# One fixed list of steps for all four batches of an attention and Fourier-mixing kernel

## Chip, core and metric

The kernel runs on one core of one Trainium2 chip. The metric is the device time of one execution in microseconds. Before the change the median of three runs is 622.02 us (621.33 to 622.77). The profiled execution took 623.03 us; its span, from the first to the last instruction, is 621.2 us.

## What is computed

Gated linear attention over 4 batches of 8 heads (768 tokens, 48 channels each), then a Fourier mixing block on the heads laid side by side (384 channels), a normalisation and two projections (384 to 1536 to 384).

```python
f = 1.0 / (1.0 + np.exp(-f_logit))
for t in range(S):
    state = f[:, :, t, :, None] * state + np.einsum('bhd,bhe->bhde', k[:, :, t], v[:, :, t])
    y[:, :, t] = np.einsum('bhd,bhde->bhe', q[:, :, t], state)
...
X = np.fft.fft(np.fft.fft(x, axis=1), axis=2)
u = x + np.real(X).astype(np.float32)
un = (u - mu) / np.sqrt(var + 1e-06)
ch = np.maximum(un @ w_ch1, 0.0) @ w_ch2
return (u + ch).astype(np.float32)
```

The weights arrive as 64-bit numbers and are turned into 32-bit ones on the chip.

## The kernel before

**Attention** works on 16 units of two heads each, four to a batch: `u = 4 b + hp`. A unit is a Python generator (`attention`, then `outputs`, then `fold`) of 13 steps, and each call of `next` records one of them:

1. `expln`: two ACT functions on the gate g;
2. DVE's scan of the gates over the tokens (L277) and the small `deep`;
3. three ACT exponentials;
4. the products of q and of k with them on DVE (L289, L290);
5. the scores `sc` on PE (L303);
6. their masking on DVE (L310, `at`);
7. `st`: k turned by PE (L448) and copied out by ACT;
8. `ds`: the states' increments on PE (L459);
9. DVE's scan of the states (`stt`, L467);
10. and 11. the outputs `y` on PE (L479, L486), copied out by ACT;
12. `yt`: turned by PE (L505) and copied by ACT into the batch's x;
13. `fold`: sums and differences of x on DVE and POOL, the input of the Fourier step. For a batch's last unit (hp = 3) all of it is on DVE.

**fnet** takes one batch: four products `z` with the table of cosines (L587), `mid` and three `mix` products (L618, L603) with their additions into x, and for each of 6 tiles of 128 tokens the moments, the normalised tile `un` (L636) and its turning `pt` on PE (L639), copied into `unT`. z, mid, mix and the first three pt are called the front of a batch here. Then the projections follow in two halves of 3 tiles: 12 groups `up` (L671, each with a Relu on ACT into h) and 3 tiles `po` (L681, 12 matmuls of 128x384 each, which read all 12 h), an addition into x (L685) and the store.

**Stores.** Tiles 0 and 4 of a batch go to the output by SP's DMA queue (L563); tile 4 in two pieces, of 1 row and of 127 rows. Tiles 1, 2, 3 and 5 go by an indirect DMA of POOL (L557), whose target rows are not known to the recording layer, so each store waits for the one before it.

**Weights.** 24 blocks of 384 KB of words (`raw`, three buffers) are loaded by SP (L235) and converted by two DVE steps (L198, L199), two ACT steps (L208, L209) and an addition of POOL (L211). `size_of` (L259) loads each block a second time and takes the smallest magnitude in it; the 24 minima, with two figures of the attention, decide a flag. If the flag is set, all is computed again by slower steps in a branch at the program's end.

**What sets the order.** Each engine runs its instructions in one order. Up to the middle of batch 0's projections that order is the list ORDER: a digit is one step of that unit, C converts a block, F is one step of fnet, L a load, T the loads of the cosine tables, S their sorting. After it a loop over PATTERN steps three units at a time and puts between them whole pieces of fnet: four up groups at a time, a whole po tile. fnet of a batch can only be called when the one before has ended. The flag is computed at the end (L760 to L770), behind the last po.

PE has two PSUM buffers for z, mix, pt, up and po together, two for sc, st, ds and yt, and one for y.

Of the kernel before, what the change touches and what calls it, by code (L numbers as in the profile page):

```python
# [19 lines left out]

PATTERN = ((2, 0), (1, 0), (1, 1), (1, 0), (2, 1), (2, 0), (1, 0), (1, 1), (1, 0),
           (0, 1), (0, 0), (0, 0), (-1, 1))
# [5 lines left out]

ORDER = (
# [8 lines left out]
def kernel(  # L38
# [105 lines left out]
    def tables():  # L144


        nc.sync.dma_start(out=tab[:, 0], in_=seq_tab[:, 0])
# [8 lines left out]
        nc.sync.dma_start(out=tab[0:1, 0, 1], in_=seq_tab[64:65, 1, 1])  # L156
# [73 lines left out]
    raws, done = [], [0]  # L230
# [24 lines left out]
    def size_of(i):  # L255


        if wide:
            nc.vector.tensor_reduce(small[:, i:i + 1], words(i)[:, :, 1].bitcast(F32), mybir.AxisListType.X,  # L259
                                    ALU.min, apply_absolute_value=True)  # L260

    def attention(u, x_all):
# [28 lines left out]
        if u:  # L291
            load(u + 3, "f", "k")
# [145 lines left out]
    def outputs(u, x_all, AT, Q, K, te, T=None):  # L438
# [61 lines left out]
        load(u + 4, "q", "v")  # L500
# [3 lines left out]
        for c, i in enumerate((0, 1, 4, 2, 3, 5)):  # L504
            nc.tensor.transpose(ps[:, c * 128:c * 128 + R], to[:, i], ident[:R, :R])  # L505
        nc.scalar.copy(
            x_all[:, :, hp * 2 * D:(hp + 1) * 2 * D].rearrange("t c (r e) -> t c r e", r=2),
            ps[:, :NCH * 128].rearrange("t (c r k) -> t c r k", r=2, k=64)[:, :, :, :D])
        yield
        fold(u, x_all)  # L510
# [53 lines left out]

    def fnet(b, x, again=False):
# [13 lines left out]
        for T in (1, 3, 0, 2):  # L579
# [11 lines left out]
            yield True  # L591
# [40 lines left out]
        unT = p2.tile([128, 3, 3 * 128], F32, tag="unT", name=f"unT{b}_0")  # L632

        def turn(c):
            un = p2.tile([128, DM], F32, tag="un", name=f"un{b}_{c}")
# [4 lines left out]
            nc.scalar.copy(unT[:, :, c % 3 * 128:(c % 3 + 1) * 128],  # L640
                           pt[:, :DM].rearrange("p (k t) -> p k t", k=3))

        for c in range(3):
# [5 lines left out]
            if c == 0:  # L649
                nc.vector.tensor_copy(x[0:1, 3], row[0:1])  # L650
            else:
                turn(c - 1)
            yield True
        turn(2)
        yield True

        for half in range(2):
            if half:
                for c in range(3, NCH):
                    moments(c)  # L660
                deviation(slice(3, NCH))
                unT = p2.tile([128, 3, 3 * 128], F32, tag="unT", name=f"unT{b}_1")
                for c in range(3, NCH):
                    turn(c)
            h1 = []
            for m in range(NF):
                if b == 1 and not again:
                    size_of(half * NF + m)
# [7 lines left out]
                yield m % 4 == 3  # L676
            for i in range(3):
                c = 3 * half + i
                po = ps_f.tile([128, 512], F32, tag="f", name=f"po{b}_{c}")
                for m in range(NF):  # L680
                    nc.tensor.matmul(po[:, :DM], lhsT=h1[m][:, i * 128:(i + 1) * 128], rhs=w2[:, m],  # L681
                                     start=(m == 0), stop=(m == NF - 1))
                    if c == 0 and m in (3, 7):
                        yield False
                nc.vector.tensor_tensor(x[:, c], po[:, :DM], x[:, c], ALU.add)  # L685
                store(b, c, x[:, c])
                yield True

    x_of, units, behind = {}, {}, []
    steps = [0] * (B * HP)

    def step(u):
        if not 0 <= u < B * HP:
            return
        b, hp = divmod(u, HP)
        if u not in units:
            if b not in x_of:  # L700
                x_of[b] = p2.tile([128, NCH, DM], F32, tag="x", name=f"x{b}")
            units[u] = attention(u, x_of[b])
        steps[u] += 1
        if units[u] and next(units[u], units) is units:
            units[u] = None
            if hp == HP - 1:
                behind.append(fnet(b, x_of.pop(b)))

    def fill(n=1, small_steps=False):

        while n and behind:
            ended = next(behind[0], None)
            if ended is None:
                behind.pop(0)
            elif ended or small_steps:
                n -= 1

    tile_of = {"g": g_t, "k": k_t, "q": q_t}
    with tc.manual_schedule():
        for word in ORDER.split():  # L720
            kind = word[0]
            if kind.isdigit():
                step(int(word))
            elif kind == "F":
                fill(1, small_steps=True)
            elif kind == "C":
                weights()
            elif kind == "R":
                fetch(int(word[1:]))
            elif kind == "L":  # L730
                load(int(word[1]), *word[2:])
            elif kind == "G":
                gap(*(tile_of[name[0]][int(name[1])] for name in word[1:].split(",")))
# [14 lines left out]
    for u, n in ((k - 2, 10), (k - 1, 4), (k, 1)):  # L748
        while steps[u] < n:
            step(u)  # L750
# [104 lines left out]
```

## Time and profile before

| what | us | share of the span |
|---|---|---|
| profiled execution, its own time | 623.03 | |
| its span | 621.2 | 100% |
| PE busy (3450 matmul records) | 554.5 | 89% |
| PE's weight loads, beside the matmuls | 361.4 | 58% |
| DVE busy | 239.4 | 39% |
| ACT busy | 195.2 | 31% |
| POOL busy | 100.7 | 16% |
| bytes moved by DMA | 44.27 MB | |

A product of 32-bit numbers shows as two matmul records, a turning as one. Matmul ends are modelled, so records overlap a little; lengths are therefore taken from pieces in which the same kind of matmul runs without a break. PE and PEld name the matmuls and the weight loads of the same engine. "Granted clock" is the share of TensorE's full clock that was granted.

### The profile page before, as it was taken

Reading aid. Unit: us, or ns where it says so; the run is one execution under the profiler, and the core shown is the slowest. Engines: PE = TensorE matmul, PEld = TensorE weight load, DVE = VectorE, ACT = ScalarE, POOL = GpSimd, SP = SyncE. Lnnn points to the kernel's source line nnn. Section 1 sums busy time; section 2 is a strip of 40 time slices with the busy share of each in tenths; the row PEclk is TensorE's granted clock in tenths of the full one; section 3 lists DMA queues with packets and bytes.
Section 4 is the critical chain, followed back from the end, with each engine's and each line's share of the span. In section 5 each row is a group of like instructions: output and inputs, shape, how many; then the busy total and the mean of one; then the engine's idle time right before and its main releaser. Section 6 shows DMA issues by size and latency. Waiting matters only on the chain.

```text
span 621.2 us, 8567 instructions
## 1 busy us (share of the span) xinstructions
PE 554.5 (89%) x3450; PEld 361.4 (58%) x3450; DVE 239.4 (39%) x431; ACT 195.2 (31%) x441; POOL 100.7 (16%) x147
## 2 busy tenths in 40 slices
PE   2865769997999979999999998999999969999993
PEld 1655546654556767655655677656655645555551
DVE  7869896209234587700420359201200350000000
ACT  5766556533311446420321224310221022102200
POOL 5445232225000113300210101100100000000000
PEclk9997788999899979999999999999999988999998
DMA  8959373323880343101100100000000000000000
GB/s 234 254 163 237 100 199 114 112 89 104 274 256 18 109 126 89 46 0 33 45 0 20 35 24 1 1 0 26 15 1 14 13 14 0 1 25 13 1 13 31
DMA packets 18113, 44.27 MB, mean 71 GB/s; under 512 B 2958, under 2 KB 4304, under 8 KB 18064
## 3 DMA queue, kind: packets, MB, share of 16 engines
q1 hardware_dynamic: 16960, 40.09, 22.8%
q0 software_dynamic: 1104, 3.54, 1.5%
q8 instruction: 29, 0.48, 0.3%
q14 instruction: 20, 0.16, 0.1%
HBM read 38.90 MB, written 4.72 MB: 70 GB/s over the span
## 4 chain that ended last, share of the span: by engine, by line
PE 73%; DVE 11%; DMA 9%; issue 3%; ACT 1%; POOL 1%; SPq 1%; POOLq 0%; DVEq 0%; ACTq 0%
PE up L671 31%; PE po L681 26%; PE z L587 3%; DMA raw<-in_w_ch_dram 3%; PE mix L603 2%; PE y L479 2%; DVE W L277 2%; DMA g<-in_qkf_dram 2%; PE sc L303 2%; PE y L486 2%; DMA out_dram<-x 2%; PE pt L639 2%; DMA tab<-in_seq_tab_dram 1%; DVE at L310 1%; PE yt L505 1%
## 5 line engine op out<-in xcount | busy, mean ns | idle before, releaser
L671 PE MATMUL up<-unT,w 128*128 128x384 f32 x576 | 195.5, 499 | 1.1 <-ACT unT L640 1.1
L681 PE MATMUL po<-w,h 128*128 128x384 f32 x576 | 189.2, 488 | 0.0
L671 PEld LDWEIGHTS up<-unT,w 128*128 128x128 f32 x576 | 110.8, 195 | 78.2 <-issue 5.7
L681 PEld LDWEIGHTS po<-w,h 128*128 128x128 f32 x576 | 108.7, 190 | 74.8 <-issue 1.1
L685 DVE TENSOR_TENSOR x<-po,x 128x384 f32<-128x384 f32 x24 | 13.4, 557 | 252.2 <-PE po L681 252.2
L674 ACT ACTIVATE h<-up 128x384 f32<-128x384 f32 x96 | 47.0, 490 | 133.7 <-PE up L671 133.7
L557 POOL DMA_INDIRECT out_dram<-x,place x16 | 17.0, 1060 | 354.5 <-DVE x L685 301.2
L303 PE MATMUL sc<-q,W 48*64 48x128 f32 x768 | 32.4, 296 | 22.6 <-DVE W L290 17.1
L303 PEld LDWEIGHTS sc<-q,W 48*64 48x64 f32 x768 | 26.3, 145 | 25.5 <-DVE W L290 13.9
L211 POOL TENSOR_TENSOR w<-w,raw 128x384 uint32<-128x384 uint32 x24 | 28.9, 1204 | 53.9 <-ACT raw L209 34.4
L310 DVE COPY_PREDICATED at<-causal,sc 128x768 f32<-128x768 uint32 x32 | 31.6, 1026 | 14.3 <-PE sc L303 14.0
L479 PE MATMUL y<-at,v 128*64 128x128 f32 (+1 forms) x384 | 31.3, 300 | 1.1 <-ACT yT L499 0.7
L479 PEld LDWEIGHTS y<-at,v 128*64 128x64 f32 (+1 forms) x384 | 25.7, 145 | 6.3 <-issue 4.5
L277 DVE TENSOR_TENSOR_SCAN W<-g,bound 112x768 f32<-112x768 f32 x16 | 27.9, 1747 | 1.9 <-issue 1.0
L450 ACT COPY kT<-st 128x560 f32<-128x560 f32 x16 | 10.0, 627 | 51.0 <-PE st L448 50.8
L639 PE MATMUL pt<-ident,un 128*128 128x128 f32 x72 | 13.8, 319 | 12.1 <-DVE un L636 8.9
L495 ACT COPY yT<-y 112x254 f32<-112x254 f32 x16 | 5.8, 364 | 57.3 <-PE y L486 57.3
L467 DVE TENSOR_TENSOR_SCAN stt<-ds,te 112x288 f32<-112x288 f32 x16 | 12.0, 751 | 27.7 <-PE ds L459 27.7
L640 ACT COPY unT<-pt 128x384 f32<-128x384 f32 x24 | 11.2, 478 | 35.1 <-PE pt L639 35.0
L486 PE MATMUL y<-q,stt 48*48 48x128 f32 x320 | 21.4, 276 | 0.8 <-DVE stt L467 0.8
L259 DVE TENSOR_REDUCE small<-raw 128x1 f32<-128x384 f32 x24 | 13.1, 551 | 21.5 <-DMA raw<-in_w_ch_dram 21.5
L486 PEld LDWEIGHTS y<-q,stt 48*48 48x48 f32 x320 | 18.1, 159 | 5.3 <-issue 3.0
(116 smaller groups left out, 525.2 us busy)
## 6 DMA issues: line engine op xcount, KB each, us to landing
raw<-in_w_ch_dram SPq DMA_DIRECT2D x48, 384.0 KB
v<-in_v_dram SPq DMA_DIRECT2D x16, 288.0 KB
g<-in_qkf_dram SPq DMA_DIRECT2D x32, 144.0 KB
k<-in_qkf_dram SPq DMA_DIRECT2D x32, 144.0 KB
q<-in_qkf_dram SPq DMA_DIRECT2D x32, 144.0 KB
out_dram<-x SPq DMA_DIRECT2D x4, 192.0 KB
out_dram<-x SPq DMA_DIRECT2D x4, 190.5 KB
tab<-in_seq_tab_dram SPq DMA_DIRECT2D x1, 386.0 KB
```

The source lines that it names most:

```text
L211: nc.gpsimd.tensor_tensor(bits, bits, lo, ALU.add)
L277: nc.vector.tensor_tensor_scan(W, g, bound[:R], 0.0, ALU.add, ALU.min)
L303: nc.tensor.matmul(ps[64 * s:64 * s + 64, r, i * C:(i + 1) * C], lhsT=W[ROWS[r], o + 64 * s:o + 64 * s + 64], rhs=Q[ROWS[r], o:o + C], sta ...
L310: nc.vector.copy_predicated(AT[:, :, half], causal.bitcast(U32).unsqueeze(1).unsqueeze(1).to_broadcast([128, 2, NCH // 2, C]), ps[:, :, :N ...
L479: nc.tensor.matmul(y[FILL[r], c * C:(c + 1) * C], lhsT=vt[:, c, r * D:r * D + (64 if r == 0 else D)], rhs=AT[:, r, c], start=(c % 4 == 0), ...
L486: nc.tensor.matmul(y[ROWS[r], c * C:(c + 1) * C], lhsT=st[ROWS[r], :, c - 1], rhs=Q[ROWS[r], c * C:(c + 1) * C], start=False, stop=True, s ...
L557: nc.gpsimd.indirect_dma_start(out=out.rearrange("b s d -> (b s) d"), out_offset=bass.IndirectOffsetOnAxis(ap=place[:, b, i:i + 1], axis=0 ...
L587: nc.tensor.matmul(z[:, cols], lhsT=src[:, j, lo:hi], rhs=tab[:, t, T % 2, cols], start=(i == 0), stop=(i == len(parts) - 1), skip_group_c ...
L639: nc.tensor.transpose(pt[:, kt * 128:(kt + 1) * 128], un[:, kt * 128:(kt + 1) * 128], ident)
L671: nc.tensor.matmul(pp[:, :3 * 128], lhsT=w1[:, kt, m * 128:(m + 1) * 128], rhs=unT[:, kt], start=(kt == 0), stop=(kt == 2))
L674: nc.scalar.activation(h, pp[:, :3 * 128], AF.Relu)
L681: nc.tensor.matmul(po[:, :DM], lhsT=h1[m][:, i * 128:(i + 1) * 128], rhs=w2[:, m], start=(m == 0), stop=(m == NF - 1))
```

## The change

ORDER now holds the whole program, 533 words, and PATTERN with its loop is gone. Its words name the batch (F0 to F3), and fnet is cut finer: every up group is a step, and every po tile three. The turnings are a generator of their own (H), the minima a word (c) that reads the block already loaded for the conversion and then issues the next block's load, and every load is a word (L). The flag is a word (M).

```diff
+    "Gq0 L0v Gq2 Gk2 Gq3 I L0f 0 Gk1 Gk0 L1f L0q Gq1 0 L1k i 1 L0k R Z 0 L1q 1 0 1 C C L3fk c 0 0 0 L2f "
...
@@ tables
-        nc.sync.dma_start(out=tab[:, 0], in_=seq_tab[:, 0])
+        nc.sync.dma_start(out=tab[:, 0, 0], in_=seq_tab[:, 0, 0])
+        nc.sync.dma_start(out=tab[1:128, 0, 1], in_=seq_tab[1:128, 0, 1])
+        nc.sync.dma_start(out=tab[0:1, 0, 1], in_=seq_tab[64:65, 1, 1])
...
@@ weights, sizes
             single(dst, raws[i])
-            fetch()
...
+    def sizes():
+        i = looked[0]
         if wide:
-            nc.vector.tensor_reduce(small[:, i:i + 1], words(i)[:, :, 1].bitcast(F32), mybir.AxisListType.X,
+            nc.vector.tensor_reduce(small[:, i:i + 1], raws[i][:, :, 1].bitcast(F32), mybir.AxisListType.X,
                                     ALU.min, apply_absolute_value=True)
+            fetch()
+        looked[0] += 1
...
@@ attention, outputs
-        if u:
-            load(u + 3, "f", "k")
...
-        load(u + 4, "q", "v")
+        if te is None:
+            load(u + 4, "q", "v")
...
@@ fnet
+        def turns():
+            for c in range(NCH):
+                if c == 3:
+                    for i in range(3, NCH):
+                        moments(i)
+                    deviation(slice(3, NCH))
+                    yield
+                turn(c)
+                yield
+
+        behind[b] = turns()
...
-                if b == 1 and not again:
-                    size_of(half * NF + m)
...
-                yield m % 4 == 3
-            for i in range(3):
+                yield
+            for i in ((0, 1, 2), (0, 2, 1))[half]:
...
-                    if c == 0 and m in (3, 7):
-                        yield False
+                    if m in (3, 7):
+                        yield
...
@@ the end
+            elif kind == "M":
+                flag = judge()
     tc.no_sync_barrier()
-    k = 6
-    while steps[k - 2] >= 13 and steps[k - 1] >= 10 and steps[k] >= 4:
-        k += 1
...
-    while any(units.values()) or behind or k < B * HP:
-        for age, n in PATTERN:
-            step(k - age)
-            fill(n)
-        k += 1
```

`judge` holds the lines that computed the flag at the end before. In the second half of each batch the po tiles now run in the order 3, 5, 4.

What it moves shows on three engines. On PE, at the turn from batch 2 to batch 3, where the row before the first is the last po tile of batch 2 (z3_1 to z3_2 are the four z of batch 3, mid3 and mix3 follow, pt3_0 to pt3_2 are its turnings). Before:

```order
L587 MATMUL z3_2_3372<-tab_108,xc_102 96x192
L618 MATMUL mid3_3381<-cd_109,zz3_3352 1x97
L618 MATMUL mid3_3381<-cd_109,zz3_3352 1x96
L603 MATMUL mix3_0_3388<-cd_109,zz3_3352 128x193 x2
L603 MATMUL mix3_0_3388<-cd_109,zz3_3352 128x192 x2
L603 MATMUL mix3_1_3401<-cd_109,zz3_3352 128x193 x2
L603 MATMUL mix3_1_3401<-cd_109,zz3_3352 128x192 x2
L639 MATMUL pt3_0_3415<-ident_110,un3_0_3413 128x128 x3
L603 MATMUL mix3_2_3420<-cd_109,zz3_3352 64x193 x4
L603 MATMUL mix3_2_3420<-cd_109,zz3_3352 64x192 x4
L639 MATMUL pt3_1_3438<-ident_110,un3_1_3436 128x128 x3
L639 MATMUL pt3_2_3445<-ident_110,un3_2_3443 128x128 x3
```

and now (up2_1_3 is the fourth up group of batch 2's second half):

```order
L690 MATMUL up2_1_3_3229<-unT2_1_2935,w1_106 128x384 x3
L633 MATMUL mid3_3237<-cd_109,zz3_3196 1x97
L633 MATMUL mid3_3237<-cd_109,zz3_3196 1x96
L618 MATMUL mix3_0_3243<-cd_109,zz3_3196 128x193 x2
L618 MATMUL mix3_0_3243<-cd_109,zz3_3196 128x192 x2
L690 MATMUL up2_1_4_3256<-unT2_1_2935,w1_106 128x384 x3
L690 MATMUL up2_1_5_3262<-unT2_1_2935,w1_106 128x384 x3
L618 MATMUL mix3_1_3268<-cd_109,zz3_3196 128x193 x2
L618 MATMUL mix3_1_3268<-cd_109,zz3_3196 128x192 x2
L618 MATMUL mix3_2_3280<-cd_109,zz3_3196 64x193 x4
L618 MATMUL mix3_2_3280<-cd_109,zz3_3196 64x192 x4
L690 MATMUL up2_1_6_3296<-unT2_1_2935,w1_106 128x384 x3
```

The whole front of batch 3 moved from behind batch 2's last po into its second half: up groups of batch 2 stand between its products, three more up groups (to up2_1_9) stand ahead of its three turnings, and two up and three po tiles of batch 2 behind them.

On DVE, in the stretch of batch 0's mix products, ahead of the first up (small is the array of minima, raw4 to raw7 the blocks), stand now:

```order
L209 TENSOR_SCALAR w1_106<-raw6_488 128x384
L210 SCALAR_TENSOR_TENSOR w1_106<-raw6_488,w1_106 128x384
L270 TENSOR_REDUCE small_113<-raw4_342 128x1
L321 COPY_PREDICATED at1_94<-causal_95,sc5_0_764 128x2x384
L321 COPY_PREDICATED at1_94<-causal_95,sc5_1_777 128x2x384
L270 TENSOR_REDUCE small_113<-raw5_390 128x1
L270 TENSOR_REDUCE small_113<-raw6_488 128x1
L478 SCALAR_TENSOR_TENSOR stt4_856<-ds4_845,te0_98 112x288
```

The minima, which ran on DVE beside batch 0's second half before (where the blocks were loaded again), stand among the conversions and the units' steps now: 8 of 24 ahead of the first up, 21 ahead of the second po.

On SP's queue, the loads of the cosine tables. Before:

```order
L147 DMA tab_108<-in_seq_tab_dram 128x772
L156 DMA tab_108<-in_seq_tab_dram 1x386
L159 DMA wave0_281<-in_dim_tab_dram 97x384
L160 DMA wave1_282<-in_dim_tab_dram 63x384
L161 DMA wave1_282<-in_dim_tab_dram 33x384
L142 DMA q3_92<-in_qkf_dram 48x768 x2
```

and now:

```order
L157 DMA tab_108<-in_seq_tab_dram 128x386
L158 DMA tab_108<-in_seq_tab_dram 127x386
L159 DMA tab_108<-in_seq_tab_dram 1x386
L170 DMA wave0_611<-in_dim_tab_dram 97x384
L171 DMA wave1_612<-in_dim_tab_dram 63x384
L172 DMA wave1_612<-in_dim_tab_dram 33x384
L152 DMA q1_90<-in_qkf_dram 48x768 x2
L148 DMA v5_671<-in_v_dram 128x576
```

The table's first half no longer comes in one transfer whose first row is then loaded anew; what stands behind it on the queue is now unit 5's q and v (q1 is the buffer of unit 5), where it was unit 3's q.

More of the change, by code (lines that the diff above doesn't have):

```diff
@@ L229 @@
     wide = w_ch1.dtype != F32
-    raws, done = [], [0]
+    raws, done, looked = [], [0], [0]
     def words(i):
@@ L682, in fnet @@
                                      start=(m == 0), stop=(m == NF - 1))
-                    if c == 0 and m in (3, 7):
-                        yield False
+                    if m in (3, 7):
+                        yield
                 nc.vector.tensor_tensor(x[:, c], po[:, :DM], x[:, c], ALU.add)
                 store(b, c, x[:, c])
[L687 to L707, printed above, removed]
@@ L719 @@
+    tile_of = {"k": k_t, "q": q_t}
     with tc.manual_schedule():
         for word in ORDER.split():
-            kind = word[0]
+            kind, n = word[0], int("0" + "".join(c for c in word if c.isdigit()))
             if kind.isdigit():
-                step(int(word))
+                if n not in units:
+                    units[n] = attention(n, lambda b=n // HP: x_all(b))
+                next(units[n], None)
             elif kind == "F":
-                fill(1, small_steps=True)
+                if n not in fronts:
+                    fronts[n] = fnet(n, x_of.pop(n))
+                next(fronts[n], None)
+            elif kind == "H":
+                next(behind[n], None)
```

89 lines of the change are left out of this document (40 added, 49 removed), and 19 rows, old and new, of the table ORDER.

## The prediction

> **What bounds the kernel now.** I read the busy time by stretch first, cut at the places where PE's work changes kind, because an average over the whole span hides which engine sets the pace where. Columns: stretch, its length, busy time of PE, PEld, DVE, ACT and POOL with instruction counts, granted clock, DMA share, GB/s.
>
> ```profile
> 0.00:94.60 94.60, 56.97 (x735) 47.21 (x736) 79.37 (x122) 57.56 (x122) 41.03 (x76) 0.87 0.75 200
> 94.60:205.80 111.20, 107.55 (x430) 64.06 (x428) 44.28 (x79) 38.26 (x76) 20.54 (x23) 0.95 0.44 137
> 205.80:254.30 48.50, 42.20 (x586) 34.26 (x585) 37.54 (x71) 25.96 (x67) 9.53 (x12) 0.93 0.34 93
> 254.30:362.70 108.40, 107.69 (x545) 66.12 (x543) 29.02 (x51) 25.44 (x55) 13.62 (x14) 1.00 0.08 26
> 362.70:389.60 26.90, 24.95 (x322) 19.92 (x319) 18.97 (x41) 11.55 (x35) 3.84 (x6) 1.00 0.03 9
> 389.60:494.60 105.00, 105.00 (x472) 63.95 (x471) 16.39 (x35) 17.72 (x43) 7.31 (x11) 1.00 0.03 10
> 494.60:611.00 116.40, 109.70 (x371) 65.74 (x369) 12.90 (x33) 18.75 (x46) 3.84 (x4) 0.96 0.03 10
> 611.00:621.20 10.20, 0.41 (x3) 0.09 (x2) 0.89 (x3) 0.00 (x0) 0.96 (x1) 0.78 0.11 35
> ```
>
> To 94.6 us, where the first `up` matmul starts, DVE is busy 79.4 us: it sets the pace there. After that PE does, except where it waits for a batch's turn from attention to projections. PE's busy time does not say how much of itself it wasted, since a matmul at a low clock or waiting in the pipe counts as busy. So I price PE's work from undisturbed pieces in the chain of waits (start, length, what; an x48 of L303 is a whole unit, x46 has two records missing):
>
> ```profile
> 564.39 23.49 PE up L671 x72
> 587.88 15.49 PE po L681 x48
> 431.87 1.31 PE sc L303 x46
> 372.63 0.50 PE st L448 x5
> 362.08 0.78 PE ds L459 x16
> 364.32 1.46 PE y L479 x23
> 77.95 1.26 PE y L486 x20
> 353.75 0.57 PE yt L505 x6
> 494.77 5.25 PE z L587 x28
> 500.74 1.52 PE mix L603 x8
> 382.81 1.48 PE mix L603 x16
> 443.42 0.48 PE pt L639 x3
> 433.18 7.94 PE po L681 x24
> ```
>
> and, from the groups by line (count, busy, mean ns of one, idle before):
>
> ```profile
> L618 PE MATMUL mid<-cd,zz 97*1 97x97 f32 (+1 forms) x16 | 2.3, 244 | 0.9 <-ACT zz L590 0.8
> ```
>
> Half a batch's up is 23.5 us and one of its six po tiles 7.74. A unit of attention is 1.37 (sc, x48) + 0.50 + 0.78 + 1.46 + 1.26 + 0.57 = 5.94 us. A batch's front (z, mid, mix, three pt) is 5.25 + 2.3 / 4 + 2 x 1.52 + 1.48 + 3 x 0.48 = 11.8, its other three pt 1.4. In all 8 x 23.5 + 24 x 7.74 + 16 x 5.94 + 4 x 13.2 = 522 us. PE ends at 611.0, so **89 us are lost** before it and 10.2 follow it.
>
> Counting what stands in each stretch gives the loss by place. Before 94.6: four units, most of a fifth, the start of a sixth and front 0, 42.8 of work, 51.8 lost. 94.6 to 205.8: 101.4 of work, 9.8 lost. 205.8 to 254.3: four units, 0.8 us more and front 1, 36.4, so 12.1 lost. 254.3 to 362.7: 106.8 of work, 1.6 lost. 362.7 to 389.6: two units and front 2, 23.8, so 3.1 lost. 389.6 to 494.6: 104.0 of work, 1.0 lost. 494.6 to 611.0: 11.8 + 2 x 23.5 + 6 x 7.74 + 1.4 = 106.7, so 9.7 lost, nearly all at front 3 (18.7 us up to the next up, with nothing beside it) and in the slow first up group behind it.
>
> **The change part by part.** The arithmetic stays; the steps get another order. Four terms.
>
> *Up to the first up* DVE's work changes. From the order: 8 minima more, 5 and 6 fewer of the two conversions, one scan with its small add, one state scan, three pairs of statistics more.
>
> ```profile
> L259 DVE TENSOR_REDUCE small<-raw 128x1 f32<-128x384 f32 x24 | 13.1, 551 | 21.5 <-DMA raw<-in_w_ch_dram 21.5
> L198 DVE TENSOR_SCALAR w<-raw 128x384 uint32<-128x384 uint32 x24 | 9.2, 384 | 6.9 <-DMA raw<-in_w_ch_dram 6.8
> L199 DVE SCALAR_TENSOR_TENSOR w<-raw,w 128x384 uint32<-128x384 uint32 x24 | 17.7, 738 | 0.8
> L277 DVE TENSOR_TENSOR_SCAN W<-g,bound 112x768 f32<-112x768 f32 x16 | 27.9, 1747 | 1.9 <-issue 1.0 <-PE st L448 0.9
> L278 DVE TENSOR_TENSOR deep<-g,W 112x5 f32<-112x5 f32 x16 | 5.4, 341 | 0.4
> L467 DVE TENSOR_TENSOR_SCAN stt<-ds,te 112x288 f32<-112x288 f32 x16 | 12.0, 751 | 27.7 <-PE ds L459 27.7
> L625 DVE BATCH_NORM_STATS2 bs<-x 128x6 f32<-128x384 f32 x24 | 12.8, 547 | 0.1
> L626 DVE BATCH_NORM_AGGREGATE mv<-bs 128x2 f32<-128x6 f32 x24 | 3.8, 168 | 0.1
> ```
>
> 8 x 0.551 - 5 x 0.384 - 6 x 0.738 + 1.747 + 0.341 + 0.751 + 3 x 0.715 = +3.05 us. DVE sets the pace, so the first up moves from 94.6 to 97.65, with 3.5 us more of PE's work (ds, y of unit 5) done ahead of it. The loads move too, on SP's queue: the table now comes in pieces of 128, 127 and 1 rows, ahead of the waves and of unit 5's q and v. Before, this place cost a wait:
>
> ```profile
> 33.15 0.32 SPq L161 DMA_DIRECT2D wave<-in_dim_tab_dram  x1
> 33.51 0.80 SPq L142 DMA_DIRECT2D q<-in_qkf_dram  x2
> ...
> 43.27 0.96 DVE L289 TENSOR_TENSOR q<-q,g 112x768 f32<-112x768 f32 x1 [3.84 <-DMA q<-in_qkf_dram]
> ```
>
> The q issued at 33.5 behind the waves ended DVE's wait at 43.27, 3.84 us of it idle. In the new order a wait of the same kind can stand before unit 5's product, with some 15 us of DVE work between the table's issue and it. I take it as equal, 0; the bounds are -3.8 (no wait) and +9.7 (the whole time of a 127-row transfer, below).
>
> *From the first up to the second po* stand now, besides up0 and one po, the rest of unit 4 and 5, nearly all of 6 and 7, 15 conversions and 13 minima. PE: 45.1 us. DVE, by its rows: 13 x 0.551 + 14 x 0.384 + 15 x 0.738 + some 14.6 for the units' scans, products and masks = 38. ACT, summed in the same way, comes to about 40, conversions for nearly half of it. Three engines are almost level, and each serves the others in a fixed order, so some loss is sure. Bounds: 1 (254.3 to 362.7 lost 1.6 in 107) and 15 (205.8 to 254.3, where DVE and PE were level too, lost 12.1 on 36.4 of work, a third). I take 6, nearer to the first, because up and po, whose inputs are ready, stand between the units' steps here and stood nowhere in that stretch.
>
> *The rest.* Left for PE are 522 - 42.8 - 3.5 - 45.1 = 430.6 us. The turns from attention to projections that cost 12.1, 3.1 and 9.7 are now spread among up groups of the batch ahead: z of batch 3 stands between up groups of batch 2, its pt too, and PE can go on into up of batch 3 with no wait. What is late next there is the pt itself: each needs un from DVE and two PSUM buffers to be emptied. I put 1 us on each of three fronts; 3.1 (what 362.7 to 389.6 lost with only attention beside it) bounds each above, 0 below. Elsewhere PE loses as from 254.3 to 362.7 and 389.6 to 494.6, 2.6 on 211: 5.3. The finer order changes from attention to projections 30 times in place of 19, at 0.2 each (the po at 433.18, behind sc, took 7.94 in place of 7.74): 2. The second load of the weights, 24 x 384 KB, goes; it ran under up and po, so it frees nothing on this path by itself (0).
>
> ```profile
> 603.40 0.57 DVE x L685
> ...
> 604.25 9.71 DMA out_dram<-x
> ```
>
> ```profile
> 606.00:610.00 4.00, 4.00 (x14) 2.31 (x13) 0.00 (x0) 0.00 (x0) 0.00 (x0) 1.00 0.06 22
> ```
>
> ```profile
> 614.76 0.96 POOL L557 DMA_INDIRECT out_dram<-x,place  x1 [17.31 <-DMA out_dram<-x]
> out_dram<-x,place POOLq DMA_INDIRECT x1, 3.0
> ```
>
> *The end.* Before, the last po was tile 5, and its store only waited some 2 us for tile 4's, which takes 9.71: 10.2 us from PE's end to the end of the span. Now tile 4 is last. While it moves, one sixteenth of the DMA engines' time is busy (0.06 in the row of the stretch). From PE's end: 0.1 to the addition, 0.85 from its start to the transfer's (603.40 to 604.25), 9.71: 10.7 until it has landed, and the closing waits behind. From the last landing before, POOL's store at 614.76 + 3.0, to the end they took 3.4; a landing on SP's queue with POOL long done is not in this trace, so the bounds are 0.5 (a few semaphore steps) and 3.4, and I take 1.7, between them: **12.4, which is 2.2 worse**. The flag set earlier saves nothing: its matmul stood at PE's end, and the landing of tile 4 (604.25 + 9.71 = 613.96) and the store behind it came later.
>
> The Trainium skill, DMA: Bandwidth & Descriptors, section "Why a DMA increments its semaphore by 16 and not by 1", says that such a transfer is split over the largest number of engines up to 16 that divides its rows, and that 127 rows go to one. The row of the stretch agrees. By that rule the table's new piece of 127 rows goes to one engine as well, which speaks against this edit: what is issued behind it would land some 9.7 us later, 19.8 after its issue (10.1 before, 33.15 to 43.27) against the 15 us of DVE work, a wait of 4.8 in place of 3.84 and a sum of 603.9; if the piece spreads, the wait is covered and the sum is 599.1.
>
> **Sum.** 97.65 + 45.1 + 6 + 430.6 + (3 + 5.3 + 2) = 589.7 for PE's end; + 12.4 = 602.1 of span. The profiled run took 623.03 for a span of 621.2, so 1.83 lies around it, and it stands 1.0 over the median of 622.02: 602.1 + 1.83 - 1.0 = 602.9.
>
> **Rivals.** (a) The level stage costs what its upper bound says: 15 in place of 6 and, since the same chain feeds the next stage, some 3 more: 615. For it: every engine there is in a fixed order. Against: ready work lies between. (b) The head gets tighter: DVE was idle 15 of its first 94.6 us, and if half of that closes, and the level stage loses 2, the time is 603 - 7.5 - 4 = 591. For it: the new order alternates units more finely. Against: nothing in the trace says that those gaps came from the order rather than from loads and latency. (c) Slower, by one mechanism: the word blocks starve. Three buffers hold 24 blocks; each is now released only after its minimum on DVE, and the third part of the first po needs block 23. By the sums above, the last 13 fetches must fit between about 91 and 148 us, 4.4 each. It decides once a fetch takes 6.4 us on average: then po is late by 26 us, and the time is 629; it passes 623.3 at 6.0. Against: with three in flight that is 19 us for one block, where the loads held up behind the waves took 10.1 and a block's conversions and minimum some 3 (rows above, and the two ACT steps and POOL's addition beside them). (d) The gains are given back by waits that the order fixes, and the time stays at 622: 19 us of new loss spread over the PE stage, against 2.6 on 211 where PE had work ready.
>
> **How the numbers follow.** Forecast (594 to 609): 0.66. (a) 0.14, (b) 0.12, (d) 0.03, (c) 0.05. The range leaves out the ends of (a) and (b), and holds the bounds of the unknown costs as far as they don't all fall together: 588 to 616. A measurement tells 0.2%, 1.2 us, from no change. Faster: 0.92 (forecast, a, b). Within 0.2%: 0.03. Slower: 0.05.
>
> **What would show it.** Right: the first up at 95 to 101 us; the second po at 146 to 153; from there no gap of PE over 1 us at a batch's turn, and the granted clock at 1.00; PE's end near 590; tile 4's store last, with some 12 us after PE. Wrong: PE waiting for `w` in the first po (c); DVE idle on a load of q at unit 5 for more than 4 us (the table); gaps before pt or st in the PE stage (d).

## The result and the profile after

The changed kernel takes **586.94 us** (median of 4 runs, 586.5 to 587.41) against 621.67 in runs of the kernel before beside it: a ratio of 0.9445, 95% interval 0.9418 to 0.9471. The profiled run took 586.55 for a span of 584.8. Times are medians; one of the six executions of the kernel called "and less ahead of turning 2" below took 917.97 us, and is left out. Forecast were 602.9, between 588 and 616: the direction was right, the gain of 35 us nearly twice the 19 that were forecast, and the time lies just below the range. Busy time by stretch of the kernel after, cut at its first up, its second po and PE's last matmul (columns as in the first view of the prediction):

```profile
0.00:92.10 92.10, 58.63 (x800) 48.25 (x800) 76.23 (x126) 52.13 (x113) 34.08 (x70) 0.91 0.67 174
92.10:138.30 46.20, 46.20 (x360) 30.32 (x359) 38.73 (x62) 36.83 (x80) 20.35 (x21) 1.00 0.50 142
138.30:572.20 433.90, 431.55 (x2295) 271.78 (x2293) 125.48 (x243) 104.55 (x249) 36.15 (x57) 1.00 0.09 28
572.20:584.80 12.60, 0.00 (x0) 0.00 (x0) 0.56 (x1) 0.00 (x0) 0.00 (x0) 0.65 0.05 18
```

From the first up on PE is busy almost without a break: the first number behind the length equals the length in the second row and misses it by 2.35 us in the third. The granted clock is 1.00 in both; before, it was 0.93 to 0.96 in the stretches that lost 9 to 12 us. What PE still waits for in those 480 us (total, times, longest):

```profile
PE up L690 <- ACT h L693: 0.6, 2, 0.3
PE up L690 <- DVE x L676: 0.5, 1, 0.5
PE mix L618 <- ACT h L693: 0.5, 1, 0.5
PE pt L656 <- ACT h L693: 0.5, 2, 0.3
```

With the prediction's 522 us of work, PE lost 51.8 us ahead of the first up and 37.3 between it and PE's end before the change; now it loses 45.8 and 4.4. **33 of these 39 us lie behind the first up**; the longer end takes some 2.4 back. Ahead of the first up there is a new wait on DVE, and SP's own issue of two loads in front of it takes long:

```profile
42.40 0.29 SPq L158 DMA_DIRECT2D tab<-in_seq_tab_dram  x1
43.72 3.08 SPq L159 DMA_DIRECT2D tab<-in_seq_tab_dram  x1
...
47.22 6.27 SPq L171 DMA_DIRECT2D wave<-in_dim_tab_dram  x1
...
54.85 0.91 SPq L152 DMA_DIRECT2D q<-in_qkf_dram  x2
```

```profile
64.92 0.96 DVE L302 TENSOR_TENSOR q<-q,g 112x768 f32<-112x768 f32 x1 [7.50 <-DMA q<-in_qkf_dram]
```

At the end tile 4's addition and store follow PE, and nothing else:

```profile
570.72 1.45 PE L700 MATMUL po<-w,h 128*128 128x384 f32 x4
...
572.21 0.56 DVE L704 TENSOR_TENSOR x<-po,x 128x384 f32<-128x384 f32 x1 [7.18 <-PE po L700]
572.79 0.52 SPq L576 DMA_DIRECT2D out_dram<-x  x2
```

### The profile page after: what moved, and what is told of

Read it like the earlier page. It is cut to its first block, busy times and chain, and to the rows that moved or that the text cites. A ratio compares the mean times of both kernels' runs of the same rounds, so it can differ in the third digit from the quotient of the medians.

```text
span 584.8 us, 8503 instructions
## 1 busy us (share of the span) xinstructions
PE 536.4 (92%) x3450; PEld 350.4 (60%) x3450; DVE 241.0 (41%) x431; ACT 193.5 (33%) x441; POOL 90.6 (15%) x147
## 4 chain that ended last, share of the span: by engine, by line
PE 84%; DMA 3%; DVE 3%; ACT 3%; SPq 2%; issue 2%; POOL 1%; ACTq 0%; DVEq 0%; POOLq 0%
PE up L690 33%; PE po L700 32%; PE z L602 4%; PE sc L314 3%; PE y L490 3%; PE y L497 2%; PE mix L618 2%; DMA q<-in_qkf_dram 2%; PE pt L656 1%; PE ds L470 1%; PE yt L517 1%; SPq L171 1%; DMA v<-in_v_dram 1%; PE st L459 1%; DMA g<-in_qkf_dram 1%
## 5 line engine op out<-in xcount | busy, mean ns | idle before, releaser
L690 PEld LDWEIGHTS up<-unT,w 128*128 128x128 f32 x576 | 106.8, 190 | 71.7 <-issue 1.2
L314 PE MATMUL sc<-q,W 48*64 48x128 f32 x768 | 29.1, 302 | 27.7 <-DVE W L303 23.1
L314 PEld LDWEIGHTS sc<-q,W 48*64 48x64 f32 x768 | 24.3, 149 | 33.0 <-issue 15.7
L222 POOL TENSOR_TENSOR w<-w,raw 128x384 uint32<-128x384 uint32 x24 | 27.5, 1148 | 52.2 <-ACT raw L220 41.0
L490 PE MATMUL y<-at,v 128*64 128x128 f32 (+1 forms) x384 | 27.0, 294 | 0.0
L490 PEld LDWEIGHTS y<-at,v 128*64 128x64 f32 (+1 forms) x384 | 23.2, 140 | 4.2 <-issue 3.4
L302 DVE TENSOR_TENSOR q<-q,g 112x768 f32<-112x768 f32 x16 | 16.7, 1041 | 20.3 <-ACT g L295 12.8
L292 POOL COPY deep<-W 112x1 f32<-112x1 f32 x16 | 5.4, 338 | 123.4 <-DVE W L290 123.2
L618 PE MATMUL mix<-cd,zz 96*128 96x192 f32 (+5 forms) x128 | 18.4, 331 | 0.7 <-ACT h L693 0.5
L210 DVE SCALAR_TENSOR_TENSOR w<-raw,w 128x384 uint32<-128x384 uint32 x24 | 17.8, 742 | 0.8
```

Of the source, the lines that this page charges most:

```text
L210: nc.vector.scalar_tensor_tensor(bits, hi, 0xC0000000, bits, ALU.bitwise_and, ALU.bitwise_or)
L222: nc.gpsimd.tensor_tensor(bits, bits, lo, ALU.add)
L314: nc.tensor.matmul(ps[64 * s:64 * s + 64, r, i * C:(i + 1) * C], lhsT=W[ROWS[r], o + 64 * s:o + 64 * s + 64], rhs=Q[ROWS[r], o:o + C], sta ...
L490: nc.tensor.matmul(y[FILL[r], c * C:(c + 1) * C], lhsT=vt[:, c, r * D:r * D + (64 if r == 0 else D)], rhs=AT[:, r, c], start=(c % 4 == 0), ...
L618: nc.tensor.matmul(mix[rows, o], lhsT=zz[:rows_of[T], T, j:j + rows.stop - rows.start], rhs=cd[:rows_of[T], T, :NQ - odd], start=(i == 0), ...
L690: nc.tensor.matmul(pp[:, :3 * 128], lhsT=w1[:, kt, m * 128:(m + 1) * 128], rhs=unT[:, kt], start=(kt == 0), stop=(kt == 2))
```

## The experiments

Fourteen kernels. The table gives, from each profiled run, the first up, the time from there to the end of PE's last matmul (with the flag last, to the end of its last po), what follows to the end of the span, and the ratio of the times to the kernel before, run on the same chip. In the kernel before the last matmul is the flag's and ends at 611.4; the prediction counts from 611.0.

| kernel | first up | to PE's end | behind | span | ratio (95%) |
|---|---|---|---|---|---|
| before | 94.6 | 516.8 | 9.8 | 621.2 | 1 |
| **after** | 92.1 | 480.1 | 12.6 | 584.8 | 0.9445 (0.9418 to 0.9471) |
| old order, new code | 103.9 | 515.9 | 12.4 | 632.1 | 1.0148 (1.01 to 1.0197) |
| new up to first up | 93.7 | 522.8 | 12.4 | 628.9 | 1.0103 (1.0073 to 1.0133) |
| old up to first up | 109.7 | 480.1 | 12.7 | 602.5 | 0.9682 (0.9636 to 0.9729) |
| coarse up and po | 92.2 | 501.6 | 12.7 | 606.4 | 0.9793 (0.9735 to 0.9851) |
| front 3 behind batch 2 | 91.7 | 485.4 | 12.6 | 589.7 | 0.9541 (0.9495 to 0.9586) |
| no minima | 88.9 | 479.8 | 12.6 | 581.3 | 0.9393 (0.9348 to 0.9439) |
| two conversions ahead | 97.7 | 480.1 | 12.7 | 590.5 | 0.952 (0.9476 to 0.9565) |
| old start | 94.6 | 480.1 | 12.6 | 587.3 | 0.9437 (0.9407 to 0.9467) |
| table late | 86.6 | 480.1 | 12.6 | 579.3 | 0.9335 (0.9289 to 0.9381) |
| table whole | 88.8 | 480.1 | 12.8 | 581.7 | 0.9368 (0.9326 to 0.9409) |
| flag last | 92.4 | 479.2 | 12.6 | 584.2 | 0.9426 (0.9383 to 0.947) |
| table late, tile 4 first | 85.4 | 480.1 | 7.2 | 572.7 | **0.9227** (0.9195 to 0.9259) |
| and less ahead of turning 2 | 83.9 | 482.7 | 7.2 | 573.8 | 0.9253 (0.9217 to 0.9289) |
| and table whole | 85.5 | 480.1 | 7.5 | 573.1 | 0.9222 (0.9195 to 0.9249) |

### The order before, in the new code

```diff
-    with tc.manual_schedule():
-        for word in ORDER.split():
...
+    with tc.manual_schedule():
+        run(ORDER.split("X")[0])
     tc.no_sync_barrier()
+    run(ORDER.split("X")[1])
```

ORDER holds the steps of the old ORDER, an X, and the steps that the old planner took, with each `c` behind its `C`.

> The code after the change, with the order of steps before (the first part fixed, the rest left to the planner and to the framework's reordering), each minimum right behind its block's conversion, so that there is no second load of the weights. 17 minima then stand ahead of the first up (17 x 0.55 = 9.4 us of VectorE), the table comes in three pieces and tile 4 is stored last (+2.4). Theory A, the prediction's price of 0 for the second load: 621.7 + 9.4 + 2.4 = 633, with the stretch of batch 1's front losing its 12 us as before. Theory B, the second load kept SP's queue from issuing the next units' loads and so made that loss: about 623, and units 8 to 11 wait for no load. If the minima find room in VectorE's idle 15 us, either figure is up to 9 lower.

632.67 us, where theory A has 633, and at batch 1's front the same wait stands with the second load and without it. First the kernel before, then this one (total, times, longest):

```profile
PE st L448 <- DVE xc L550: 2.8, 1, 2.8
```

```profile
PE st L459 <- DVE xc L563: 2.8, 1, 2.8
```

**Dropping the second load was worth no more than 1 us by itself** (516.8 and 515.9 us from the first up to PE's end), as the prediction had priced it. Some 46 us lie between the two orders in the same code.

That the first up comes 9.2 us later, as 17 minima of 0.55 would make it, is partly luck. Only 15 of the 17 run ahead of it. DVE is busy 85.58 us up to there in place of 79.37, which is 6.2 more, and idle 3.1 us longer. Its longest wait for a q, issued behind the table that now comes in three pieces, is 8.9 us in place of 3.84.

### The new order up to the first up, the old one behind it

ORDER holds the new words up to the first up, then what is left of the old ones. At the joint:

```diff
-... C H0 5 C L8qv F0 c F0 C c 7 F0 5 F0 6 C ...
+... C H0 5 C L8qv c c C c C c C c C c C c C c ...
```

> The new order up to the first up, then the order before (planner and framework's reordering) for all that is left. Theory A, the gain arises where the order differs: the stretches behind the first up lost 37.3 us before and 4.4 now, so about 587 + 33 = 620 less a few us for units 5 and 6 that stand further. Theory B, the head's order makes the gain, because units ahead of their time keep the turns covered: 590 to 600.

629.39 us. At the joint, where the old order has conversions next, stands a wait that neither kernel has:

```profile
110.60 1.65 PE L691 MATMUL up<-unT,w 128*128 128x384 f32 x2 [12.16 <-ACT h L694]
```

Without it the time would be near 617, an estimate (629.39 less 12.16), near theory A, and theory B is out. By that estimate the new head is worth some 5 of the 35 us against the kernel before, but some 15 of the 46 against the old order in the same code, which has 15 minima ahead of the first up in place of 8.

### The old order up to the first up, the new one behind it

```diff
-... 5 C c 5 C c F0 F0 C c 4 F0 F0 C c 5 ...
+... 5 C c 5 C c 6 6 5 5 5 H0 5 F0 F0 7 F0 5 F0 6 ...
```

> The order before up to the first up (with 17 minima in it instead of 8 and 17 conversions instead of 10), then the new order. Theory A, VectorE's recorded work ahead of what up waits for sets the first up: it comes at about 104, and the end 12 later less the 2 to 3 us that the level stage saves by having 9 minima and 7 conversions less: about 596. Theory B, loads and latency set the head: first up at 95 to 97, end at 586 to 589.

603.71 us, above both theories. The first up comes at 109.7, later than the 104 of theory A because the new order's steps that the old head lacks (unit 5's last ones, statistics) now stand between. From here to the change, with the new head, are 16.8 us; from the old order in the same code to here are 29. The rows of the two middle stretches:

```profile
109.70:155.90 46.20, 46.20 (x359) 30.32 (x358) 23.85 (x39) 28.27 (x64) 9.21 (x12) 1.00 0.21 61
155.90:589.80 433.90, 431.59 (x2295) 271.81 (x2293) 125.48 (x243) 104.69 (x249) 36.28 (x57) 1.00 0.09 28
```

This is the clearest reading of the study. Behind the first up the time to PE's end is 480.1 us, as in the change. From the first up to the second po DVE has 23.85 us to do in place of 38.73, ACT 28.27 in place of 36.83, POOL 9.21 in place of 20.35, and the stretch is **46.20 us long in both**. The prediction's "three engines almost level" named busy times rightly and drew the wrong conclusion: with the steps woven as finely as now, PE alone sets that stretch.

### Coarse up and po

From batch 0's second half on, each up group of a block stands at the place of the block's fourth, each third of a po at the place of its last, for example at batch 3's front:

```diff
-F3 F2 F3 F3 F3 F2 F3 F2 F2 F3 F3 F2 F2 F2 F2 H3 H3 H3
+F3 F3 F3 F3 F2 F2 F2 F2 F3 F3 F3 F2 F2 F2 F2 H3 H3 H3
```

> The new order, with up groups from batch 0's second half on in blocks of four and each po whole, as the order before had them, all else in place. Theory A, the fine interleaving keeps PE busy at the batches' turns: 3 to 10 us come back, 590 to 597, as gaps before z, mix and pt. Theory B, it is enough that ready up groups stand near the fronts, the grain does not matter: 586 to 589. If switching between attention and projections costs PE, fewer changes even gain 1 to 2 us.

609.16 us, 22 more than the change and twice what theory A allowed at most. All of it lies behind the second po, where the stretch grows from 433.9 to 455.4:

```profile
138.40:593.80 455.40, 435.52 (x2295) 273.77 (x2293) 124.67 (x244) 104.82 (x249) 36.16 (x57) 0.99 0.09 26
```

```profile
PE pt L656 <- DVE un L653: 7.3, 3, 3.6
PE z L602 <- DVE se L559: 2.7, 1, 2.7
PE up L690 <- ACT unT L657: 2.5, 1, 2.5
PE up L690 <- DVE x L676: 2.4, 2, 1.8
```

PE is idle 19.9 us there in place of 2.35 and busy 4 more, for the same matmuls in the same numbers, at a granted clock of 0.99 in place of 1.00. The waits are the short chain from a front's product through DVE and ACT to the next one. With single up groups between its links each wait is covered; in blocks the links follow each other on PE and the blocks come too late. The edit does both, it joins the groups and moves three of four to a later place, and no run parts the two. The Trainium skill, Perfetto Trace Analysis, section "Optimization Strategy", says that where the most-contended engine changes over time, interleaving the regimes may help; these rows agree, and show that how finely it is done, and at which place, decides: both kernels interleave the same regimes.

### Batch 3's front behind batch 2's last po

```diff
-... 15 F2 F2 F2 F3 F2 F3 F3 F3 F2 F3 F2 F2 F3 F3 F2 F2 F2 F2 H3 H3 H3 F2 ...
+... 15 F2 F2 F2 F2 F2 F2 ... F2 F3 F3 F3 F3 F3 F3 F3 H3 H3 H3 F3 F3 F3 H3 ...
```

> Batch 3's front (z, mid, mix and the first three turnings) stands behind batch 2's last po, where the order before had it, all else in place. Theory A (the turn's loss comes from a front with nothing beside it): 9 to 10 us come back, 596 to 597, as gaps of PE before pt and up and a slow first up group. Theory B (the engines run ahead of PE by themselves, so most of the front is done in time): 587 to 590.

593.0 us, 6.1 more than the change; the span of the profiled run, the shortest of its four, is 4.9 longer. That is half to two thirds of theory A. The end of that front on PE:

```profile
476.06 2.36 PE L656 MATMUL pt<-ident,un 128*128 128x128 f32 x9 [2.68 <-DVE un L653]
478.99 5.47 PE L690 MATMUL up<-unT,w 128*128 128x384 f32 x10 [0.57 <-ACT unT L657]
```

So one uncovered turn costs 5 to 6 us. Behind the first up of the program PE is idle 2.7 us longer than in the change, and busy 2.6 longer. The second part is the clock: it is granted at 0.53 from 476.0 to 479.0 us, at 0.50 to 481.5, at 0.75 to 484.5 and at 1.00 behind that. The kernel before shows the same behind its front 3, 0.54 from 513.3 to 518.0 us and 1.00 behind; this is the "slow first up group" of the prediction. The mechanism is the forecast's, but the place of the front accounts for only about half of the 9.7 us that the old order lost here.

### No minima, and two conversions moved ahead

```diff
-            nc.vector.tensor_reduce(small[:, i:i + 1], raws[i][:, :, 1].bitcast(F32), mybir.AxisListType.X,
-                                    ALU.min, apply_absolute_value=True)
             fetch()
```

> The 24 minima over the weight words are left out (the flag then sees sizes of 1.0); the blocks are fetched where they were. Theory A (VectorE's work ahead of the last un sets the first up; behind it PE has work enough and VectorE's load does not matter): eight minima less ahead of it, first up 4 us earlier, near 88, and the end as much and no more: 583. Theory B (VectorE, PE and ScalarE are level from the first up to the second po): the 13 minima of that stage count too, 579 or less. Theory C (loads set the head): 587.

583.9 us: theory A, with 3.2 us in place of 4 at the first up. Eight minima are 4.3 us, but up to the third un DVE's busy time fell by only 2.8, as other operations ran longer. The 13 minima behind it saved 0.3 at most.

```diff
-... 4 5 H0 H0 5 5 H0 C H0 5 C L8qv F0 ...
+... 4 5 C C H0 H0 5 5 H0 H0 5 L8qv F0 ...
```

> The ninth and tenth conversions stand ahead of batch 0's first turning instead of behind its third. Theory A (only what stands on VectorE ahead of the last un that up waits for counts): first up 1.8 to 2.2 later, near 94, end 588.5 to 589. Theory B, the count of the prediction (all that is recorded ahead of up): nothing changes, 587.

592.09 us, the first up 5.6 us later: theory A's direction, at almost three times its size. 1.7 us of that stand already at the mix products ahead of the moved words, and are not explained. The two conversions then hold up the first un on DVE, which starts at 90.83 in place of 87.42:

```profile
89.11 0.35 DVE L209 TENSOR_SCALAR w<-raw 128x384 uint32<-128x384 uint32 x1
89.49 0.56 DVE L210 SCALAR_TENSOR_TENSOR w<-raw,w 128x384 uint32<-128x384 uint32 x1
89.97 0.35 DVE L209 TENSOR_SCALAR w<-raw 128x384 uint32<-128x384 uint32 x1
90.35 0.56 DVE L210 SCALAR_TENSOR_TENSOR w<-raw,w 128x384 uint32<-128x384 uint32 x1
90.83 1.57 DVE L653 TENSOR_SCALAR un<-x,mv,rstd 128x384 f32<-128x384 f32 x2
```

and in the change:

```profile
87.42 0.86 DVE L653 TENSOR_SCALAR un<-x,mv,rstd 128x384 f32<-128x384 f32 x2
```

That makes 3.4 us. The two un take 0.7 us longer as well, and PE waits for the second. The last 1.5 are PE's: between the second turning and the first up it has the same work as in the change, and takes 4.7 us for it in place of 3.2, at a granted clock of 0.64 from 93.0 to 97.7 us, where the change has 1.00.

### The program's start

```diff
-Gq0 L0v Gq2 Gk2 Gq3 I L0f 0 Gk1 Gk0 L1f L0q Gq1 0 L1k i 1 ...
+I Gk0 Gq0 Gk2 Gq2 Gq3 L0v L0f Gk1 Gq1 Z 0 L1f L0k L0q 1 0 ...
```

> The steps up to the table's loads (some 33 us) in the order of before, with the minimum behind each conversion, the rest in the new order. Theory A (the order of the first loads and exponentials lets VectorE start earlier, 4 us less idle in the first 40 us): the first up comes 3 to 4.5 us later, near 96, and the end as much, 590 to 591.5. Theory B (the gain ahead of the first up arises behind that, in how units 2 to 5 and the front are woven): first up at 91.5 to 93, end 586 to 588.

588.09 us. Between the theories, and unclear by time, since its ratio is that of the change itself; in the profiled runs the first up comes 2.5 us later, but this was the longest of its four, and the median spans are only 1.2 us apart (586.35 and 585.15). Five kernels with the change's words up to there had the first up between 91.7 and 93.7. By 33 us DVE has worked 28.93 us in the change and 26.95 with the old start. So 1 to 2.5 us of the head's gain arise in its first 33 us, not clear of the spread.

### The table's place and form

```diff
-... 2 4 1 T 3 2 3 4 5 4 L5qv 6 ...
+... 2 4 1 3 2 3 4 5 4 L5qv T 6 ...
```

> The table's loads and the waves stand behind the loads of unit 5's q and v instead of ahead of them. Theory A (the table and the waves, queued ahead, make VectorE's wait of 7.5 us at unit 5's product): the wait goes, the first up comes 5 to 7 us earlier, near 86, and the end as much: 580 to 582. Theory B (the wait only moves, to the first step that needs the table or the waves, the copies ahead of z): first up at 90 to 92, end 585 to 587.

581.07 us: theory A. The 7.5 us of DVE's wait are gone, and the first up comes 5.5 earlier. With the old form at the place that the change gave it:

```diff
-        nc.sync.dma_start(out=tab[:, 0, 0], in_=seq_tab[:, 0, 0])
-        nc.sync.dma_start(out=tab[1:128, 0, 1], in_=seq_tab[1:128, 0, 1])
-        nc.sync.dma_start(out=tab[0:1, 0, 1], in_=seq_tab[64:65, 1, 1])
+        nc.sync.dma_start(out=tab[:, 0], in_=seq_tab[:, 0])
...
+        nc.sync.dma_start(out=tab[0:1, 0, 1], in_=seq_tab[64:65, 1, 1])
```

> The table as before the change, in one transfer of 128 rows and a row set behind it, at the new place. Theory A (the piece of 127 rows holds up SP's queue by its whole length): VectorE's wait at unit 5's product falls from 7.5 us to 2 to 4, end 582 to 584. Theory B (the waves of 97, 63 and 34 rows do it, the table's form does not matter): wait and end as they are, 586 to 588.

583.12 us: theory A, with a wait of 2 to 4 us. SP's queue at that place, to be read against the lines of the change above:

```profile
48.08 0.29 SPq L166 DMA_DIRECT2D tab<-in_seq_tab_dram  x1
48.41 0.25 SPq L169 DMA_DIRECT2D wave<-in_dim_tab_dram  x1
48.70 0.74 SPq L170 DMA_DIRECT2D wave<-in_dim_tab_dram  x1
...
49.90 0.78 SPq L152 DMA_DIRECT2D q<-in_qkf_dram  x2
```

```profile
60.80 1.06 DVE L301 TENSOR_TENSOR q<-q,g 112x768 f32<-112x768 f32 x1 [3.07 <-DMA q<-in_qkf_dram]
```

The same issue of a wave takes 0.74 us in place of 6.27, q goes out 5 us earlier, and DVE waits 3.07 in place of 7.50. The edit changes a second thing: SP waits 5.4 us here for the whole table to land, since the row behind it overwrites a part of it, and only then issues the waves. So the three pieces cost these 5 us; that the 127 rows alone do it is not shown.

### Flag last, and the best order found

```diff
-... F3 F3 c M F3 F3 ...
+... F3 F3 c F3 F3 ... F3 F3 M
```

> The flag's steps stand at the end, behind the last po, as before the change. Theory A (their path lies beside tile 4's store and its landing): nothing, 587. Theory B (the loads of the flag's value come behind the last stores and the end waits for them): 1 to 3 us more.

586.43 us: nothing, as forecast. Then the table late and, in each second half, tile 4 as the first po:

```diff
-            for i in ((0, 1, 2), (0, 2, 1))[half]:
+            for i in ((0, 1, 2), (1, 0, 2))[half]:
```

> The table behind unit 5's loads, as in the experiment before, and in each second half tile 4 as the first po and tile 5 as the last, so that the one-queue store of tile 4 runs under the two others. Theory A: head 5.5 us less as measured, and from PE's end 0.1 + 0.6 for the addition, 1.0 for POOL's issue, 3.0 for the transfer and 3.4 to the end, 8 in place of 12.6: 586.9 - 5.5 - 4.6 = 577. Theory B (the end waits for something else than the last store, the closing part is as long as before): 581.

**574.2 us, 12.7 below the change** and 7.7% below the kernel before (0.9227, 0.9195 to 0.9259). Theory A has 577: the end is 0.8 us shorter than its 8, and the first up comes 1.2 us earlier than with the table late alone, which no edit explains. The end, 7.2 us behind PE in place of 12.6:

```profile
565.56 0.56 DVE L704 TENSOR_TENSOR x<-po,x 128x384 f32<-128x384 f32 x1 [7.18 <-PE po L700]
566.40 0.96 POOL L570 DMA_INDIRECT out_dram<-x,place  x1 [4.01 <-DVE x L704]
```

Two kernels that should better it did not. With three minima and a conversion moved behind the third turning:

```diff
-... L7qv 5 c c F0 4 4 F0 5 L6qv L8fk 6 C F0 F0 4 c 4 5 H0 H0 5 5 H0 C H0 5 C L8qv F0 c F0 C c ...
+... L7qv 5 F0 4 4 F0 5 L6qv L8fk 6 F0 F0 4 4 5 H0 H0 5 5 H0 c c C c H0 5 L8qv F0 C c F0 C c ...
```

> The same, and three minima and one conversion moved from ahead of the last turning to behind it, the two conversions after them between the first up groups. Theory A (VectorE's work ahead of the last un sets the first up, everything behind it follows at a fixed distance): 3 x 0.55 + 0.9 = 2.6 us less, 574.5. Theory B (the blocks of words are then fetched too late): the same first up, but PE waits for w in the later up groups or in the first po, 577 or more.

575.56 us, between the theories. The first up comes 1.5 us earlier in place of 2.6, and PE loses it again in a wait for a relu (h). From 80 to 133 us DVE waits 5.5 us for blocks in place of 3.9, so the conversions that stand among the relus come later:

```profile
PE up L690 <- ACT h L693: 2.3, 1, 2.3
```

And with the table in one transfer, by the edit shown for it above:

> The best kernel so far (table behind unit 5's loads, tile 4 first) with the table in one transfer of 128 rows and a row set behind it. Theory A (SP's queue is then free some 8 us earlier, but nothing behind it is awaited): as that kernel, 573.5 to 575. Theory B (the loads of units 6 and 7 behind it are awaited): 1 to 3 us less, 571 to 573.

574.44 us, theory A: where nothing behind it is awaited, the table's form costs nothing.

## Why the prediction was wrong in size

That the fine order keeps PE busy was right; three terms of the sum were mis-sized, all to the same side, and the range assumed that they would not all be.

| term | forecast | measured |
|---|---|---|
| first up | 97.65 | 92.1 |
| first up to second po | 45.1 + 6 | 46.2 |
| second po to PE's end | 430.6 + 10.3 | 433.9 |
| behind PE's end | 12.4 | 12.6 |
| around the span | 1.83 | 1.75 |
| from the profiled run to the median | -1.0 | +0.4 |

*The head, 5.6 us.* The step that failed is the count of DVE's work "ahead of" the first up, +3.05 by group means. On DVE, up waits for the third un and for no later work. The statistics of tiles 3 to 5 and conversions nine and ten are recorded ahead of up but behind that un. The windows that end with it (to 0.1 us), first of the kernel before, then after, show what counts:

```profile
0.00:92.50 92.50, 54.87 (x725) 45.24 (x726) 77.27 (x119) 56.40 (x119) 41.03 (x76) 0.88 0.75 197
```

```profile
0.00:89.30 89.30, 55.84 (x760) 45.94 (x762) 73.57 (x119) 50.81 (x110) 34.08 (x70) 0.90 0.66 171
```

DVE's busy time up to there fell by 3.7, which is 6.75 below the count. Its idle time grew by 0.5 us, from 15.2 to 15.7, and the way from the third un to up by 0.7, from 2.1 to 2.8; 6.75 less these two is the 5.55 by which the first up came before its forecast. Less than half of the 6.75 is the wrong cut: with the group means, counted up to the third un, some +0.7 would have come out, an estimate from the rows of these windows (8 minima, one scan, deep, state scan and mask more, 6 and 7 conversion steps fewer). The larger part, some 4.4, is that single operations ran shorter than their means or than before: an un 469 ns in place of 715, the second conversion step 652 in place of 744, the product of k 979 in place of 1110. Why they did is not shown.

The idle time hides two things. The table's wait grew from 3.84 to 7.50, within the bounds given; by the rule of the Trainium skill named there (DMA: Bandwidth & Descriptors, "Why a DMA increments its semaphore by 16 and not by 1") it would have been 4.8. What that estimate left out is SP's own issuing: q landed 10.1 us after its issue, much as before (9.8; the prediction's 10.1 counts from the wave ahead of it), but it was issued 13.1 us behind the table's first load in place of 9.5. So some 3 us of idle time closed elsewhere, which is rival (b)'s mechanism, and the table took them back.

*The level stage, 4.9 us.* Loss was taken as 6, on the argument that level busy times in a fixed order must collide. The stage lost 1.1. The old head shows why the argument fails and not only its size: 15 us less on DVE, 8.6 on ACT and 11 on POOL changed nothing. That PE always has an up group or a po beside the units' steps was the point; the text saw it ("ready work lies between") and still took 6 of bounds from 1 to 15, where the lower bound held.

*The rest, 7.0 us.* 3 for the fronts, 5.3 of general loss and 2 for switching; measured 3.3 in all. The general loss was carried over from stretches in which the old order placed up groups in blocks of four, so it belonged to that order and not to the work. The coarse kernel shows from the other side how much hangs on the order: with blocks, at their later places, the 3.3 become 24.8. PE's busy time of 431.55 leaves at most 1 us for switching 30 times.

*What held.* The work of 522 us and its split, within some 1 us a stretch; the second load at 0; the flag at 0; the tail at 12.4; no starving of the word blocks (rival c); no waits handed back behind the second po (d). The granted clock of 1.00 behind the second po came true, and so did one of the signs of being wrong, DVE idle for more than 4 us at unit 5. Rival (b), 591 us with a chance of 0.12, came nearest, in part by luck: the head's idle time did not close, its work shrank. It named gains in the head and the level stage together and left the rest untouched; that the second and third term follow from one cause, the fine order, and so move together, was not in the chances.

## What to carry to other kernels

Where one engine sets the time, ask at each of its waits whether a step of other work whose inputs are ready stands next in its queue, and whether there are enough of them to last as long as the wait. Where it was so here, level busy times on the helpers cost nothing. Losses measured under a coarser order must not be carried over to a finer one. Ahead of the first step of that engine's long run, count only what this step waits for, and from instances at that place where there are any, not from group means; each microsecond there moves the end by one (eight kernels here have the same 480.1 us behind it). A transfer that is slow to issue belongs behind the loads that someone waits for, and the slow store ahead of the last fast one.

## What the runs showed of the hardware that was not expected

SP's own issue of a load is not always short: 3.08 us for one row directly behind the table's piece of 127 rows, and 6.27 for the wave of 63 rows a little later, 6.90 and 6.95 in two runs with the table late. From 48 to 52 us, within the issue of 6.27, the DMA engines are busy 7 to 11% of the time. With the table in one transfer of 128 rows, whose landing SP had waited for, the 63 rows took 0.74. The Trainium skill, DMA: Bandwidth & Descriptors, section "Issuing engines are not separate DMA queues", calls the time that a sequencer takes to initiate a DMA usually small beside the DMA itself; it was not in these rows. It was in the kernel before, where the three waves were issued in 0.24 to 0.69 us each, also after SP had waited for the table (7.2 us). No run has the piece of 127 rows with such a wait behind it, so which of the two makes the issue long stays open.

A gap on PE can cost more than its own length. In three places the granted clock was low where PE went on behind a wait: 0.50 to 0.75 for some 5 us of up groups behind the uncovered front 3, 0.54 for 4.7 us at the same place of the kernel before, 0.64 for 4.7 us ahead of the first up with two conversions ahead. In the change the clock is 1.00 from the first up to PE's end. No run varies the gap alone.
